# The low part of a layer's activation taken from PSUM, on VectorE in every step

## The chip, the cores and the metric

One core of a Trainium2 chip runs the program. The metric is device time in microseconds; three runs of the kernel before gave 1035.62, 1037.53 and 1037.84 us, a median of 1037.53. The engines are named as the profile names them: PE (TensorE, with PEld for its weight loads), DVE (VectorE), ACT (ScalarE), POOL (GpSimd) and SP (SyncE, which issues the DMAs).

## The reference

A recurrent attention (`r`, `k`, `v`, `w`, `u`; 4 batches, 8 heads, 768 positions, 48 per head) gives 3072 tokens of 384 values. Two feed-forward layers follow, each 384 to 2048 to 384:

```python
h = x @ w_in
g = np.where(h >= 1, h, np.where(h <= -1, 0.0, (h + 1) ** 2 / 4))   # layer 1
y = g @ w_out
h = y @ w2_in
g = h * (1.0 / (1.0 + np.exp(-1.702 * h)))                          # layer 2
out = g @ w2_out
```

The weights arrive as float64 bits, and all is computed in float32. Each matrix product is made of three products of rounded parts: an operand is split into a high part, rounded to the matmul's type (`gh` for the activation), and a low part, the rest (`gl = g - gh`).

## The kernel before, in words

The tokens are cut into 8 tiles of 384, and the 2048 hidden values into 16 slices of 128. A **step** `s` is one slice of one tile: 128 steps of layer 1, then 128 of layer 2 (`step`, line 260). A step issues, in the order of the program:

- `gemm1` (L651): nine matmuls into a PSUM tile `hp`, the slice of `h`. Up to step 111 there are two `hp` buffers, so that `gemm1` of step s needs the buffer of step s-2 to be free; from step 112 there are four.
- the first half of the activation. In layer 1 (`relu2_a`) DVE clamps `hp` into an SBUF tile `t` (L688), and ACT squares `t` (L689); in layer 2 ACT alone takes the sigmoid (L707).
- `low_g` of step s-1 (L676): `gl = t - gh`. It goes to POOL and DVE in turn, step by step.
- one slot of attention work for the tile after this one: a window of 128 tokens passes through some twenty slots. Its DVE work is two scans (L423, L425), a copy and a product (L429, L430), a reduction (L451), two predicated copies (L474) and four small updates (L510); PE has transposes, scores and products for it (L464, L469, L498, L504); POOL has products and a selection.
- `gemm2` or `gemm3` of step s-3: nine matmuls that read `gh` and `gl` of that step (L660, L669).
- the second half of the activation. In layer 1 (`relu2_b`) DVE takes the maximum of `t` and `hp` (L701) into `t`, in layer 2 their product (L712); then ACT writes `gh`, the rounded copy of `t` (L682).
- in six steps of a tile, the conversion of a piece of layer 2's weights (two DVE instructions, L638 and L642, then ACT, POOL and a DMA), and in every other step a second slot of attention work.

A tile of steps holds three windows of attention. The attention of the first tile and steps 0 to 15 are ordered by a scheduler with its own costs; from step 16 on (`manual_schedule`) each engine takes its instructions in the order of the program, and an instruction that waits holds up all that stands behind it on its engine. Attention slots end with step 111; the last tile of layer 1 (steps 112 to 127) prepares layer 2's weights instead.

Who frees `hp` before the change: the last reader is the maximum (L701).

Of the kernel before, what the change touches and what calls it, by code (L numbers as in the profile page):

```python
# [9 lines left out]
F32 = mybir.dt.float32  # L10
# [3 lines left out]
AF = mybir.ActivationFunctionType  # L14
ALU = mybir.AluOpType
# [44 lines left out]
PRIO = True  # L60
WTS = ('wt', 'gh', 'wt', 'gl', 'wt', 'ev')
WBS = ('wb', 't')
LOW0 = (0, 1)
XL_N = 6
F0 = 0
WP0 = 400
# [5 lines left out]
BANKS = (0, 1, 2)  # L72
TAGB = {'wt': 4, 'gh': 4, 'gl': 3, 'ev': 3, 'wb': 2, 't': 3}
AHEAD = 6
LOW_E = (0, 1)
GAPS = (1, 1, 1)
GAP0 = 4
CONV0 = 2
# [23 lines left out]
def fast_path(st, tc, rkw_t, nat, v_l, w1, w2, u, out, x2_d, w2_d, flag_i, force):  # L102
    nc = tc.nc
    one = st.enter_context(tc.tile_pool(name="one", bufs=1))
    p2 = st.enter_context(tc.tile_pool(name="p2", bufs=2))
# [44 lines left out]
    def to_f32(l, n):  # L150
        todo = []
        for _ in range(n):
            i = nconv[l]
            nconv[l] += 1
            raw = staged.pop((l, i))
            tags = (WTS[i % len(WTS)], WBS[i % len(WBS)]) if l == 0 and i < N0 else ("wt", "wb")
            t = p2.tile([128, DM], I32, tag=tags[0], name="wt", bufs=TAGB[tags[0]])
            b = p2.tile([128, DM], I32, tag=tags[1], name="wb", bufs=TAGB[tags[1]])
            todo.append((i, raw[:, :, 1].bitcast(I32), raw[:, :, 0], t, b))
        wide(nc, [x[1:] for x in todo])  # L160
        for i, top, low, t, b in todo:
            if l == 1 or not CHECK_LATE:
                check_w(l, i, top)
            load_w(l)
        return [(x[0], x[3].bitcast(F32)) for x in todo]

    def split_w(i, wf):
        f, q = pieces[i]
        nc.scalar.activation(out=whi[f][q], in_=wf, func=AF.Copy)
        pat = LO0 if i < N0 else LO1  # L170
        how = pat[i % len(pat)]
        if how == "p":
            ps = hooks["ps"]()
# [11 lines left out]
    def conv_w1():  # L185
        new = to_f32(0, 2) if nconv[0] < NPC else []
        if nconv[0] <= N0:
            half.extend(new)
            new = []
        while half:  # L190
            split_w(*half.pop(0))
        half.extend(new)
# [26 lines left out]
    gq = {}  # L219
# [6 lines left out]
    def where(s):  # L226
        if s < KF * len(TILES):
            return (0, s // KF, s % KF) + TILES[s // KF]
        s -= KF * len(TILES)
        return (1, s // KF, s % KF) + TILES2[s // KF]  # L230
# [29 lines left out]
    def step(s):  # L260
        if s < NS:
            l, i, f, t0, n = where(s)
            last = l == 0 and i == len(TILES) - 1
            slots = l == 0 and not last
            if l == 0 and f == 0:
                cur[0] = i
            if l == 0 and i == 0:
                with hooks["prio"](CP1):
                    while nconv[0] < min(NPC, 2 * f + 2 + AHEAD):
                        conv_w1()  # L270
                    if nconv[0] == NPC:
                        conv_w1()
            hp = pools["h"][s % len(pools["h"])].tile([128, 512], F32, tag="h", name="hp")
            gemm1(nc, hp, n, xh[l, i], xl[l, i], f, win, whi, wlo)
            if l == 0 and ALT[f % len(ALT)] and i < ALT_N:
                t = relu2_c(nc, p2, hp, n, (None, nc.gpsimd, nc.vector)[ALT[f % len(ALT)]])
            else:
                t = (relu2_a, swish_a)[l](nc, p2, hp, n)
        if s - 1 in gq:
            low_g((nc.gpsimd, nc.vector)[(LOW_E if s >= 16 else LOW0)[s % len(LOW_E)]], p2, gq, s - 1, where(s - 1)[4])  # L280
        if s < NS:
            if slots:
                per = KF - F0 if i == 0 else KF
# [22 lines left out]
        if s < NS:  # L306
            gq[s] = (relu2_b, swish_b)[l](nc, p2, t, hp, n)
# [362 lines left out]
            i += 1  # L670


def low_g(eng, p2, gq, f, n):
    t, gh, _ = gq[f]
    gl = p2.tile([128, TN], F32R, tag="gl", name="gl", bufs=3)
    eng.tensor_tensor(out=gl[:, 0:n], in0=t[:, 0:n], in1=gh[:, 0:n].bitcast(F32), op=ALU.subtract)  # L676
    gq[f] = gh, gl


def high_g(nc, p2, t, n):  # L680
    gh = p2.tile([128, TN], F32R, tag="gh", name="gh", bufs=4)
    nc.scalar.activation(out=gh[:, 0:n], in_=t[:, 0:n], func=AF.Copy)  # L682
    return t, gh, None


def relu2_a(nc, p2, hp, n):
# [11 lines left out]


def relu2_b(nc, p2, t, hp, n):  # L700
    nc.vector.tensor_tensor(out=t[:, 0:n], in0=t[:, 0:n], in1=hp[:, 0:n], op=ALU.max)  # L701
    return high_g(nc, p2, t, n)


def swish_a(nc, p2, hp, n):
# [3 lines left out]


def swish_b(nc, p2, t, hp, n):
    nc.vector.tensor_tensor(out=t[:, 0:n], in0=t[:, 0:n], in1=hp[:, 0:n], op=ALU.mult)  # L712
    return high_g(nc, p2, t, n)


def relu2(nc, t, h):
# [147 lines left out]
```

## Time and profile before

| | |
|---|---|
| median of three runs | 1037.53 us |
| the profiled execution, its own time | 1035.07 us |
| its span | 1033.3 us |
| PE busy | 950.6 us (92%) |
| DVE busy | 604.1 us (58%) |
| ACT busy | 517.5 us (50%) |
| POOL busy | 469.6 us (45%), of which 132.0 us are 128 `gl` (L676) |
| `gl` on DVE (L676) | 81.4 us, 128 of them |
| `gh` on ACT (L682) | 133.9 us, 256 of them |

The shares are means over stages of different kinds: the attention of the first tile and the first steps up to about 170 us, steps 16 to 111 with attention beside them up to about 570 us, then the last tile of layer 1 and layer 2. They are read by stage. Starts in a timeline are us from the start of the span; "[0.53 <-DVE t L701]" at the end of a row means that the engine sat idle for 0.53 us before it, and that the instruction of line 701 on DVE ended that. On DVE and ACT an instruction may start up to 0.1 us ahead of the end of the one in front of it.

### The profile page before, as it was taken

To read this page: it belongs to the slowest core of one execution; us is meant where nothing else is said; L and a number is where in the kernel's file an instruction comes from. 1 tells how busy PE (TensorE), PEld (TensorE's weight loads), DVE (VectorE), ACT (ScalarE), POOL (GpSimd) and SP (SyncE) were. 2 spreads that over 40 slices of the span, in tenths; PEclk is the share of its full clock that TensorE was granted. 3 is DMA by queue.
4 is the path that set the end of the run, shared out by engine and by line. 5 is a ranking of instruction groups with operands and counts; after the bars stand their busy time and mean duration, and the time that the engine had idled before them with its cause. 6 is when DMAs were issued, how large, how long until landed. Compare 5 with 4: busy or idle time off the path is not lost.

```text
span 1033.3 us, 18712 instructions
## 1 busy us (share of the span) xinstructions
PE 950.6 (92%) x6976; PEld 903.7 (87%) x6976; DVE 604.1 (58%) x1007; ACT 517.5 (50%) x1221; POOL 469.6 (45%) x481
## 2 busy tenths in 40 slices
PE   4645889999999999999999999999999999999997
PEld 2434769989888988898989999999999999999997
DVE  8999984787877777778674663323232323232321
ACT  5654554565555655546653565455555433333332
POOL 6897872676676666766662342111111111111111
PEclk8756989999999999999999999999999999999999
DMA  9763422644534545434310543232323110101000
GB/s 250 203 191 107 129 56 56 188 126 128 145 103 110 147 129 142 131 103 126 101 43 5 167 153 108 62 107 62 108 62 109 30 46 1 47 2 46 15 9 27
DMA packets 52228, 100.20 MB, mean 97 GB/s; under 512 B 8608, under 2 KB 34464, under 8 KB 52128
## 3 DMA queue, kind: packets, MB, share of 16 engines
q1 hardware_dynamic: 52128, 98.91, 33.2%
q8 instruction: 57, 0.93, 0.4%
q14 instruction: 43, 0.35, 0.1%
HBM read 81.97 MB, written 15.73 MB: 95 GB/s over the span
## 4 chain that ended last, share of the span: by engine, by line
PE 57%; DVE 17%; POOL 8%; ACT 6%; issue 6%; DMA 4%; SPq 2%; POOLq 0%; ACTq 0%; DVEq 0%
PE hp L651 27%; PE acc L669 20%; PE acc L660 8%; DVE pi L423 2%; DVE t L701 2%; ACT gh L682 2%; DVE ra L474 2%; DVE pi L425 2%; DVE gl L676 1%; DVE wt L638 1%; DMA wst<-w 1%; POOL ra L437 1%; POOL rkn L426 1%; POOL wt L644 1%; DVE wt L642 1%
## 5 line engine op out<-in xcount | busy, mean ns | idle before, releaser
L676 POOL TENSOR_TENSOR gl<-t,gh 128x384 fp32r<-128x384 f32 x128 | 132.0, 1031 | 387.7 <-ACT gh L682 386.1
L682 ACT ACTIVATE gh<-t 128x384 fp32r<-128x384 f32 x256 | 133.9, 523 | 205.5 <-DVE t L701 122.9
L712 DVE TENSOR_TENSOR t<-t,hp 128x384 f32<-128x384 f32 x128 | 70.8, 553 | 218.6 <-ACT t L707 218.1
L707 ACT ACTIVATE t<-hp 128x384 f32<-128x384 f32 x128 | 63.0, 492 | 145.8 <-PE hp L651 145.8
L660 PE MATMUL acc<-gh,whi 128*128 128x384 f32 x384 | 132.4, 350 | 0.3 <-DVE ev L252 0.3
L660 PE MATMUL acc<-gl,whi 128*128 128x384 f32 x384 | 130.2, 339 | 1.2 <-DVE gl L676 1.2
L669 PE MATMUL acc<-wlo,gh 128*128 128x384 f32 x384 | 130.2, 339 | 0.0
L669 PE MATMUL acc<-whi,gh 128*128 128x384 f32 x384 | 129.9, 338 | 0.0
L660 PE MATMUL acc<-gh,wlo 128*128 128x384 f32 x384 | 129.6, 338 | 0.0
L669 PE MATMUL acc<-whi,gl 128*128 128x384 f32 x384 | 129.3, 337 | 0.0
L651 PE MATMUL hp<-xh,whi 128*128 128x384 f32 x384 | 95.9, 359 | 24.1 <-DVE t L701 23.0
L676 DVE TENSOR_TENSOR gl<-t,gh 128x384 fp32r<-128x384 f32 x128 | 81.4, 636 | 47.0 <-ACT gh L682 44.6
L689 ACT ACTIVATE t<-t 128x384 f32<-128x384 f32 x128 | 66.3, 518 | 78.7 <-DVE t L688 76.8
L701 DVE TENSOR_TENSOR t<-t,hp 128x384 f32<-128x384 f32 x128 | 70.1, 548 | 51.9 <-ACT t L689 51.1
L644 POOL TENSOR_TENSOR wt<-wt,wb 128x384 int32<-128x384 int32 x64 | 71.7, 1121 | 62.0 <-ACT wb L640 51.1
L651 PEld LDWEIGHTS hp<-xh,whi 128*128 128x128 f32 x384 | 67.8, 193 | 33.3 <-DVE t L701 29.9
L688 DVE TENSOR_SCALAR t<-hp 128x384 f32<-128x384 f32 x128 | 70.4, 550 | 41.7 <-PE hp L651 41.6
L651 PE MATMUL hp<-xl,whi 128*128 128x384 f32 x384 | 90.2, 344 | 0.0
L651 PE MATMUL hp<-xh,wlo 128*128 128x384 f32 x384 | 89.4, 341 | 0.0
L651 PE MATMUL hp<-x2l,whi 128*128 128x384 f32 x384 | 88.8, 339 | 0.0
L651 PE MATMUL hp<-x2h,wlo 128*128 128x384 f32 x384 | 88.0, 337 | 0.0
L651 PE MATMUL hp<-x2h,whi 128*128 128x384 f32 x384 | 87.4, 335 | 0.0
(106 smaller groups left out, 1944.3 us busy)
## 6 DMA issues: line engine op xcount, KB each, us to landing
wst<-w SPq DMA_DIRECT2D x96, 384.0 KB, 3.4
rk<-rkw_t SPq DMA_DIRECT2D x48, 289.7 KB, 4.9
rkn<-nat SPq DMA_DIRECT2D x24, 384.0 KB, 4.1
w_d<-wt SPq DMA_DIRECT2D x32, 192.0 KB, 3.3
w2f<-w_d SPq DMA_DIRECT2D x32, 192.0 KB, 2.5
vn<-nat SPq DMA_DIRECT2D x24, 192.0 KB, 3.0
lt<-v_l SPq DMA_DIRECT2D x48, 96.0 KB, 3.0
x_d<-ev SPq DMA_DIRECT2D x24, 192.0 KB, 2.5
```

The costliest lines, as they stand in the source:

```text
L423: nc.vector.tensor_tensor_scan(out=rr[:, WW:0:-1], data0=ws[:, WW:0:-1], data1=one_s[:, WW:0:-1], initial=0.0, op0=ALU.mult, op1=ALU.max)
L644: nc.gpsimd.tensor_tensor(out=t, in0=t, in1=b, op=ALU.add)
L651: nc.tensor.matmul(out=hp[:, 0:n], lhsT=win(a, f, kk), rhs=b[:, kk, 0:n], start=(i == 0), stop=(i == 3 * KD - 1))
L660: nc.tensor.matmul(out=acc[j][:, 0:n], lhsT=wout(a, f, j * 128, 128), rhs=b[:, 0:n], start=(f == 0 and i == 0), stop=(f == KF - 1 and i == 2))
L669: nc.tensor.matmul(out=o[:, 0:DM], lhsT=a[:, j * 128:(j + 1) * 128], rhs=wout(b, f, 0, DM), start=(f == 0 and i == 0), stop=(f == KF - 1 a ...
L676: eng.tensor_tensor(out=gl[:, 0:n], in0=t[:, 0:n], in1=gh[:, 0:n].bitcast(F32), op=ALU.subtract)
L682: nc.scalar.activation(out=gh[:, 0:n], in_=t[:, 0:n], func=AF.Copy)
L688: nc.vector.tensor_scalar(t[:, 0:n], hp[:, 0:n], scalar1=-1.0, scalar2=1.0, op0=ALU.max, op1=ALU.min)
L689: nc.scalar.activation(out=t[:, 0:n], in_=t[:, 0:n], func=AF.Square, bias=0.5, scale=0.5)
L701: nc.vector.tensor_tensor(out=t[:, 0:n], in0=t[:, 0:n], in1=hp[:, 0:n], op=ALU.max)
L707: nc.scalar.activation(out=t[:, 0:n], in_=hp[:, 0:n], func=AF.Sigmoid, scale=1.702)
L712: nc.vector.tensor_tensor(out=t[:, 0:n], in0=t[:, 0:n], in1=hp[:, 0:n], op=ALU.mult)
```

## The change

The result of the activation is written back into `hp`, in PSUM, by the second half (L701, L712). ACT reads `gh` from there. `low_g` reads `hp` from there too, on DVE in every step, and it is issued at the front of the next step, ahead of that step's `gemm1` and of its first half. POOL takes no `gl`. `hp` is now freed by `gl`. The two tables that dealt `gl` out between POOL and DVE are gone.

```diff
@@ step
+            if s - 1 in gq:
+                low_g(nc, p2, gq, s - 1, where(s - 1)[4])
             hp = pools["h"][s % len(pools["h"])].tile([128, 512], F32, tag="h", name="hp")
             gemm1(nc, hp, n, xh[l, i], xl[l, i], f, win, whi, wlo)
...
-        if s - 1 in gq:
-            low_g((nc.gpsimd, nc.vector)[(LOW_E if s >= 16 else LOW0)[s % len(LOW_E)]], p2, gq, s - 1, where(s - 1)[4])
+        elif s - 1 in gq:
+            low_g(nc, p2, gq, s - 1, where(s - 1)[4])
@@ low_g, high_g
-    t, gh, _ = gq[f]
+    hp, gh, _ = gq[f]
     gl = p2.tile([128, TN], F32R, tag="gl", name="gl", bufs=3)
-    eng.tensor_tensor(out=gl[:, 0:n], in0=t[:, 0:n], in1=gh[:, 0:n].bitcast(F32), op=ALU.subtract)
+    nc.vector.tensor_tensor(out=gl[:, 0:n], in0=hp[:, 0:n], in1=gh[:, 0:n].bitcast(F32), op=ALU.subtract)
...
-    nc.scalar.activation(out=gh[:, 0:n], in_=t[:, 0:n], func=AF.Copy)
+    nc.scalar.activation(out=gh[:, 0:n], in_=hp[:, 0:n], func=AF.Copy)
@@ relu2_b (swish_b alike, with mult)
-    nc.vector.tensor_tensor(out=t[:, 0:n], in0=t[:, 0:n], in1=hp[:, 0:n], op=ALU.max)
-    return high_g(nc, p2, t, n)
+    nc.vector.tensor_tensor(out=hp[:, 0:n], in0=t[:, 0:n], in1=hp[:, 0:n], op=ALU.max)
+    return high_g(nc, p2, hp, n)
```

Line numbers of the changed kernel that lie between line 75 and `low_g` are lower by two in part: L176 and L250 there are L178 and L252 before; L638 to L712 are the same.

**DVE, first scan place of a tile (layer 1, from step 16 on).** L423 to L425 are a window's scans, L429 and L430 its copy and product, L688 the clamp of a step, L701 its maximum, L676 its `gl`. Before:

```order
L425 SCALAR_TENSOR_TENSOR pi<-rk_160,seed 128x520
L701 TENSOR_TENSOR t<-t,hp 128x384
L688 TENSOR_SCALAR t<-hp 128x384
L676 TENSOR_TENSOR gl<-t,gh 128x384
L429 COPY pcs<-pi 128x8
L430 TENSOR_TENSOR rk_160<-rk_160,pi 128x512
L701 TENSOR_TENSOR t<-t,hp 128x384
L638 TENSOR_SCALAR wt<-wst 128x384
L642 SCALAR_TENSOR_TENSOR wt<-wst,wt 128x384
L451 TENSOR_REDUCE bb<-rkn 128x8
L688 TENSOR_SCALAR t<-hp 128x384
```

With the change:

```order
L425 SCALAR_TENSOR_TENSOR pi<-rk_160,seed 128x520
L701 TENSOR_TENSOR hp<-t,hp 128x384
L676 TENSOR_TENSOR gl<-hp,gh 128x384
L688 TENSOR_SCALAR t<-hp 128x384
L429 COPY pcs<-pi 128x8
L430 TENSOR_TENSOR rk_160<-rk_160,pi 128x512
L701 TENSOR_TENSOR hp<-t,hp 128x384
L638 TENSOR_SCALAR wt<-wst 128x384
L642 SCALAR_TENSOR_TENSOR wt<-wst,wt 128x384
L451 TENSOR_REDUCE bb<-rkn 128x8
L676 TENSOR_TENSOR gl<-hp,gh 128x384
L688 TENSOR_SCALAR t<-hp 128x384
```

Before, the clamp of the next step stood behind the maximum, and `gl` of every other step behind that clamp. Now `gl` stands directly behind the maximum whose value it takes, or behind the maximum, the weight piece and the reduction, and the clamp of the next step behind `gl`.

**DVE, second scan place of a tile**, where the scans are in a step's second slot, behind its maximum. Before:

```order
L701 TENSOR_TENSOR t<-t,hp 128x384
L638 TENSOR_SCALAR wt<-wst 128x384
L642 SCALAR_TENSOR_TENSOR wt<-wst,wt 128x384
L510 TENSOR_TENSOR us<-lt_162,kv_2208 48x192 x2
L423 SCALAR_TENSOR_TENSOR pi<-rk_161,one_s 128x520
L424 RECIPROCAL seed<-pi 128x8
L425 SCALAR_TENSOR_TENSOR pi<-rk_161,seed 128x520
L688 TENSOR_SCALAR t<-hp 128x384
L429 COPY pcs<-pi 128x8
L430 TENSOR_TENSOR rk_161<-rk_161,pi 128x512
L701 TENSOR_TENSOR t<-t,hp 128x384
```

With the change:

```order
L701 TENSOR_TENSOR hp<-t,hp 128x384
L638 TENSOR_SCALAR wt<-wst 128x384
L642 SCALAR_TENSOR_TENSOR wt<-wst,wt 128x384
L510 TENSOR_TENSOR us<-lt_162,kv_2208 48x192 x2
L423 SCALAR_TENSOR_TENSOR pi<-rk_161,one_s 128x520
L424 RECIPROCAL seed<-pi 128x8
L425 SCALAR_TENSOR_TENSOR pi<-rk_161,seed 128x520
L676 TENSOR_TENSOR gl<-hp,gh 128x384
L688 TENSOR_SCALAR t<-hp 128x384
L429 COPY pcs<-pi 128x8
L430 TENSOR_TENSOR rk_161<-rk_161,pi 128x512
L701 TENSOR_TENSOR hp<-t,hp 128x384
```

Before, the clamp of the next step was the first activation work behind the scans. Now it is the `gl` of the step whose maximum stands ahead of them.

**DVE, end of the part that the scheduler orders.** `ra_1376` and `ra_1377` are the predicated copies of one window, and the rows around them are steps of the first tile. Before:

```order
L178 TENSOR_TENSOR wlo_0_137<-wt,whi_0_105 128x384
L429 COPY pcs<-pi 128x8
L688 TENSOR_SCALAR t<-hp 128x384
L701 TENSOR_TENSOR t<-t,hp 128x384
L688 TENSOR_SCALAR t<-hp 128x384
L701 TENSOR_TENSOR t<-t,hp 128x384
L474 COPY_PREDICATED ra_1376<-mask,sc 64x512
L474 COPY_PREDICATED ra_1377<-mask,sc 64x512
L676 TENSOR_TENSOR gl<-t,gh 128x384
L688 TENSOR_SCALAR t<-hp 128x384
```

With the change:

```order
L425 SCALAR_TENSOR_TENSOR pi<-rk_161,seed 128x520
L474 COPY_PREDICATED ra_1376<-mask,sc 64x512
L688 TENSOR_SCALAR t<-hp 128x384
L642 SCALAR_TENSOR_TENSOR wt<-wst,wt 128x384
L474 COPY_PREDICATED ra_1377<-mask,sc 64x512
L676 TENSOR_TENSOR gl<-hp,gh 128x384
L176 TENSOR_TENSOR wlo_0_137<-wt,whi_0_105 128x384
L701 TENSOR_TENSOR hp<-t,hp 128x384
L537 TENSOR_TENSOR xl<-xr,xh 128x3x128
L676 TENSOR_TENSOR gl<-hp,gh 128x384
```

Ahead of the copy into `ra_1377` stand eleven maxima before (those of steps 0 to 10), and six with the change (0 to 5). The order of ACT is the same from step 16 on; POOL's loses its 128 `gl` and keeps the rest.

## Rows read from the trace of the kernel before

**Rows 1.** Windows: length; busy us (instructions) of PE, PEld, DVE, ACT, POOL; PEclk, DMA, GB/s.

```profile
130.00:156.00 26.00, 20.87 (x153) 18.20 (x152) 22.00 (x33) 13.57 (x30) 17.89 (x17) 0.87 0.24 56
300.00:400.00 100.00, 95.94 (x859) 89.38 (x858) 77.18 (x133) 54.74 (x136) 66.98 (x69) 1.00 0.45 124
700.00:800.00 100.00, 100.00 (x571) 100.00 (x570) 31.40 (x54) 51.95 (x130) 15.99 (x16) 1.00 0.28 87
```

**Rows 2.** Longest waits of PE, whole run, then 150 to 650 us.

```profile
PE hp L651 <- DVE t L701: 23.0, 22, 5.0
...
PE hp L651 <- DVE t L701: 10.7, 17, 1.2
```

**Rows 3.** Three lines of VectorE: duration ns min/median/max, first and last start.

```profile
L676 DVE TENSOR_TENSOR gl<-t,gh x128: 526/558/1379, 102.0 to 1018.4; 128x384 fp32r<-128x384 f32 x128
...
L701 DVE TENSOR_TENSOR t<-t,hp x128: 525/553/556, 99.6 to 615.3; 128x384 f32<-128x384 f32 x128
...
L688 DVE TENSOR_SCALAR t<-hp x128: 524/550/559, 97.9 to 613.9; 128x384 f32<-128x384 f32 x128
```

**Rows 4.** Timeline, first scan place of a tile: VectorE, then ScalarE, then PE.

```profile
327.70 0.56 DVE L701 TENSOR_TENSOR t<-t,hp 128x384 f32<-128x384 f32 x1
...
328.90 1.14 DVE L676 TENSOR_TENSOR gl<-t,gh 128x384 fp32r<-128x384 f32 x1 [0.18 <-ACT gh L682]
...
333.43 0.55 DVE L688 TENSOR_SCALAR t<-hp 128x384 f32<-128x384 f32 x1
...
328.35 0.53 ACT L682 ACTIVATE gh<-t 128x384 fp32r<-128x384 f32 x1 [4.91 <-DVE t L701]
...
328.31 0.80 PE L651 MATMUL hp<-xh,whi 128*128 128x384 f32 x3 [0.53 <-DVE t L701]
...
332.24 0.80 PE L651 MATMUL hp<-xh,whi 128*128 128x384 f32 x3 [0.51 <-DVE t L701]
```

**Rows 5.** Timeline, second scan place: VectorE, then PE.

```profile
345.42 0.56 DVE L701 TENSOR_TENSOR t<-t,hp 128x384 f32<-128x384 f32 x1
...
351.26 0.56 DVE L688 TENSOR_SCALAR t<-hp 128x384 f32<-128x384 f32 x1
...
348.89 0.69 PE L651 MATMUL hp<-xh,whi 128*128 128x384 f32 x3
...
353.19 0.80 PE L651 MATMUL hp<-xh,whi 128*128 128x384 f32 x3 [0.96 <-DVE t L701]
```

**Rows 6.** Timeline, third scan place: VectorE, then ScalarE, then PE.

```profile
373.56 0.55 DVE L701 TENSOR_TENSOR t<-t,hp 128x384 f32<-128x384 f32 x1
...
375.35 0.55 DVE L688 TENSOR_SCALAR t<-hp 128x384 f32<-128x384 f32 x1
...
375.99 0.53 ACT L689 ACTIVATE t<-t 128x384 f32<-128x384 f32 x1 [0.77 <-DVE t L688]
...
378.17 0.51 ACT L682 ACTIVATE gh<-t 128x384 fp32r<-128x384 f32 x1
...
374.38 0.69 PE L651 MATMUL hp<-xh,whi 128*128 128x384 f32 x3
...
377.54 0.69 PE L651 MATMUL hp<-xh,whi 128*128 128x384 f32 x3
```

**Rows 7.** Timeline of PE where it waits for GpSimd.

```profile
364.36 0.33 PE L504 MATMUL yt<-ra,lt 128*64 128x64 f32 x2 [0.77 <-POOL lt L446]
...
364.95 0.68 PE L504 MATMUL yt<-ra,lt 128*64 128x64 f32 x14 [0.26 <-POOL lt L446]
```

**Rows 8.** Timeline of VectorE, the last scan of the loop.

```profile
523.83 1.77 DVE L423 TENSOR_TENSOR_SCAN pi<-rk,one_s 128x520 f32<-128x520 f32 x1
```

**Rows 9.** Timeline near step 16: VectorE, then PE.

```profile
153.36 1.54 DVE L474 COPY_PREDICATED ra<-mask,sc 64x512 f32<-64x512 int32 x2
...
142.54 1.33 PE L651 MATMUL hp<-xh,whi 128*128 128x384 f32 x3 [3.71 <-DVE t L701]
...
171.56 0.79 PE L651 MATMUL hp<-xh,whi 128*128 128x384 f32 x3
```

More of the change, by code (lines that the diff above doesn't have):

```diff
@@ L62 @@
 WBS = ('wb', 't')
-LOW0 = (0, 1)
 XL_N = 6
@@ L74 @@
 AHEAD = 6
-LOW_E = (0, 1)
 GAPS = (1, 1, 1)
@@ L670, in gemm3, with low_g, high_g @@
             i += 1
-def low_g(eng, p2, gq, f, n):
-    t, gh, _ = gq[f]
+def low_g(nc, p2, gq, f, n):
+    hp, gh, _ = gq[f]
     gl = p2.tile([128, TN], F32R, tag="gl", name="gl", bufs=3)
-    eng.tensor_tensor(out=gl[:, 0:n], in0=t[:, 0:n], in1=gh[:, 0:n].bitcast(F32), op=ALU.subtract)
+    nc.vector.tensor_tensor(out=gl[:, 0:n], in0=hp[:, 0:n], in1=gh[:, 0:n].bitcast(F32), op=ALU.subtract)
     gq[f] = gh, gl
-def high_g(nc, p2, t, n):
+def high_g(nc, p2, hp, n):
     gh = p2.tile([128, TN], F32R, tag="gh", name="gh", bufs=4)
-    nc.scalar.activation(out=gh[:, 0:n], in_=t[:, 0:n], func=AF.Copy)
-    return t, gh, None
+    nc.scalar.activation(out=gh[:, 0:n], in_=hp[:, 0:n], func=AF.Copy)
+    return hp, gh, None
 def relu2_a(nc, p2, hp, n):
@@ L711, in swish_b @@
 def swish_b(nc, p2, t, hp, n):
-    nc.vector.tensor_tensor(out=t[:, 0:n], in0=t[:, 0:n], in1=hp[:, 0:n], op=ALU.mult)
-    return high_g(nc, p2, t, n)
+    nc.vector.tensor_tensor(out=hp[:, 0:n], in0=t[:, 0:n], in1=hp[:, 0:n], op=ALU.mult)
+    return high_g(nc, p2, hp, n)
 def relu2(nc, t, h):
```

## The prediction

> **What bounds the kernel now.** I read the busy time by stretch first, since the whole run mixes stages. In layer 2 PE is busy for the whole of its 100 us and VectorE for 31.40; in the attention steps (300 to 400 us) PE has 95.94, VectorE 77.18 and GpSimd 66.98; in the early stretch VectorE has 22.00 of 26 and PE 20.87 [rows 1]. So the end is set by PE, and what counts is how long PE stands still before about 570 us. Whatever it loses there comes out at the end, since layer 2 has nothing to win back. The list of waits names the one wait of PE that this change touches: gemm1 waits for the maximum on VectorE, the last reader of `hp`, 22 times, 23.0 us, 10.7 of it in 17 waits after 150 us [rows 2]. The timeline then shows where: behind a window's scans, when VectorE is late.
>
> **The loop.** With two `hp` buffers gemm1 of step s may start when step s-2 has let go of its buffer. That ended with the maximum. Now ACT's `gh` and VectorE's `gl` come behind it. The prices are in one place: a maximum starts at 327.70 and takes 0.56, `gh` starts at 328.35 and takes 0.53, and `gl` starts 0.02 after that [rows 4]. `gl` itself I take at 0.55, below. From the end of the maximum to the end of `gl` is 0.09 + 0.53 + 0.02 + 0.55 = 1.19 us. A step without attention takes PE 3.16 us (377.54 less 374.38 [rows 6]), and the buffer is asked for two steps later, so 1.19 us is covered where VectorE is on time. Where gemm1 already waits for the maximum, all of it shows. VectorE also can no longer use the wait for `gh`: the clamp of the next step used to stand in it, and now stands behind `gl`.
>
> **The price of a `gl` from PSUM.** No row shows this form, nor a VectorE result written to PSUM. The nearest: the clamp, which reads `hp` in PSUM, 524/550/559 ns; the maximum, with one input in PSUM, 525/553/556; `gl` now, both inputs in SBUF, 526/558 and up to 1379 [rows 3]. I take 0.55 for it, and the same for the maximum as before; the ends are 0.52 and 0.56. [...]
>
> **What each tile pays.** A tile of steps holds three windows, with their scans in three places. I walk each with the durations of the timeline and the order of the change.
>
> First place. The maximum ended at 328.26 and gemm1 started at 328.31. Now `gl` runs from 328.90 to 329.45 and gemm1 starts at 329.50: 1.19 late. The clamp behind it starts 1.2 later than now, but the old `gl` there took 1.14 [rows 4], and without it VectorE reaches the window's copy at the time it does today. The next `gl` stands where a clamp now starts, at 333.43, behind the maximum, the weight piece and the reduction: it ends at 333.98, and gemm1 starts at 334.03 instead of 332.24 [rows 4]. PE is 1.79 late.
>
> Second place. The maximum at 345.42 is followed by the weight piece, the updates and both scans, and the next clamp starts at 351.26 [rows 5]. The `gl` of that maximum is now in the clamp's place, so the buffer, free at 345.98 today, is free at 351.81. gemm1 starts at 351.86 instead of 348.89, 2.97 late. The step after it waited for VectorE at 353.19 today; PE, pushed back, gets there at 351.86 + 3.16 = 355.02, about when its own `gl` is ready. Net 1.83.
>
> Third place. Behind the maximum at 373.56 come the copy and the product, and the clamp at 375.35 [rows 6]. With `gl` in the clamp's place gemm1 starts at 375.95 instead of 374.38, 1.57 late. The clamp and the square behind it are 0.47 later. From that square to its `gh` ACT has 2.18 us of attention work (375.99 to 378.17 [rows 6]), so `gh` ends at 379.15, `gl` at 379.72, and gemm1 starts at 379.77 instead of 377.54: 2.23.
>
> What comes back: PE waits 0.77 and 0.26 us for GpSimd's update of the state [rows 7]; GpSimd has one `gl` less ahead of it there, 1.03 us (132.0 us for 128 in the table above), so I take all 1.03 off.
>
> Together 1.79 + 1.83 + 2.23 - 1.03 = 4.82 us a tile. The delays add up, since the places are steps apart and VectorE's own chain shifts with PE. The bounds: 1.8 if only the first place counts and the other two are absorbed, 7.0 if the second keeps its whole 2.97 and GpSimd gives nothing back. I take 4.8, nearest to the rows. The attention steps are six tiles; five hold all three places, the last only the first one (its scan at 523.83 is the last of the loop [rows 8]). 5 x 4.82 + 1.79 = 25.9 us.
>
> **The early part** is VectorE's. Its work hardly changes: eight `gl` more at 0.55, and those that were stretched are shorter. But `hp` is held longer, and the scheduler lets the steps fall back: ahead of the last window's second predicated copy stand six maxima instead of eleven. The copies start at 153.36 today [rows 9]; with five maxima and four clamps fewer ahead of them, some 0.5 us each, they end at about 149 to 150, and the `gl` that frees gemm1 of step 7 comes at about 147.5 to 149.5 (the lower figure if the copies go up as the order has them, straight behind the scan). From there to step 16 are nine steps at 3.16 us and 0.7 us of attention products, 29.1: step 16 at 176.6 to 178.6, instead of 171.56 [rows 9]. Against that, GpSimd has eight `gl` less in a stretch where it is nearly as full as VectorE. I take +5, with 0 and +7 as ends.
>
> **What costs nothing.** From step 112 on there are four `hp` buffers, two steps more of cover, and VectorE is at 31.40 of 100 us in layer 2 [rows 1]; another 16 `gl` of 0.55 in that stretch make it about 40. `gl` of each step is ready about two steps ahead of the matmuls that read it. If that cover went, each step would pay up to the 1.19, 128 of them: nothing points to that. The three `gl` buffers make a `gl` wait for PE's matmuls of three steps before; those end before PE starts the step whose clamp follows, so they hold nothing up. GpSimd's freed 132 us lie off the path but for the 1.03 above. No DMA and no queue is moved.
>
> **Sum.** 25.9 + 5 = 30.9 us. The profiled execution took 1035.07 us, which gives 1066.0. The median of the runs stands 2.46 above it, so I forecast **1068**. The bounds together give 5 x 1.8 + 1.8 + 0 = 10.8 (1048 on the median) and 5 x 7.0 + 1.8 + 7 = 43.8 (1081).
>
> **The rivals.**
> *Faster: GpSimd was the brake.* A VectorE instruction with two SBUF inputs is stretched when GpSimd works beside it: the old `gl` goes up to 1379 ns, the maximum, with one input in PSUM, never above 556 [rows 3]. If GpSimd's `gl` are what makes VectorE late, its lateness goes away with them, and with it PE's 10.7 us of waits after 150 us: 1027. That decides if VectorE gets more than 1.19 us earlier at the first place; the shorter `gl` gives 0.59 there, and GpSimd's long products beside it stay. [...] Chance 0.06.
> *No difference:* every added wait falls into time in which PE has its own queue, and the early part stays. The 17 waits speak against it. Chance 0.03, 1037.
> *Half of it:* only the first place counts. Chance 0.17, about 1048.
> *The clock as well.* [...] Chance 0.12.
> *That the change does not do what it says* is excluded by the order: GpSimd has no `gl` left. My forecast itself gets 0.62.
>
> **Numbers.** The range runs from 1046 to 1085, from just under the half case to just over the clock case; it leaves out the faster and the unchanged case and some tails. About 0.2% (2 us) is what a measurement can tell from no change. Slower by more: 0.62 + 0.17 + 0.12, less a little for small outcomes, 0.90; within: 0.03; faster: 0.07.
>
> **What would show it.** Right: PE's waits for gemm1 now name `gl` (L676) on VectorE and come to some 40 us or more after 150 us; the last scan of the loop starts near 523.83 + 5 + 24.1 = 553 us; step 16 starts at about 177; `gl` rows are 0.55 throughout; layer 2 has the same length. Wrong: gemm1 waits of under 15 us in the attention steps, a `gl` far from 0.55, or PE gaps in layer 2.

## The result, and the profile after

The changed kernel takes 1051.92 us (1050.43 to 1052.33); beside it, on the same chip, the kernel before took 1037.68. The ratio is 1.0139 with an interval of 1.0121 to 1.0157: 14.2 us slower. The direction was forecast and the time lies in the range, but 1068 put the move at over twice its size (30.5 us). The profiled execution of the changed kernel took 1052.25 us.

The page, busy times and two groups (`line engine op out<-in xcount | busy, mean ns | idle before, releaser`):

```profile
PE 955.0 (91%) x6976; PEld 905.5 (86%) x6976; DVE 647.7 (62%) x1135; ACT 511.6 (49%) x1221; POOL 326.4 (31%) x353
...
L676 DVE TENSOR_TENSOR gl<-hp,gh 128x384 fp32r<-128x384 f32 x256 | 142.1, 555 | 131.5 <-ACT gh L682 128.0
L682 ACT ACTIVATE gh<-hp 128x384 fp32r<-128x384 f32 x256 | 124.8, 488 | 170.1 <-DVE hp L701 91.4
```

GpSimd lost its 132 us of `gl`, and VectorE has 256 of them. The windows, beside [rows 1] (length; busy of PE, PEld, DVE, ACT, POOL; PEclk, DMA, GB/s):

```profile
130.00:156.00 26.00, 22.53 (x156) 20.55 (x157) 20.39 (x37) 10.99 (x23) 15.65 (x15) 0.87 0.21 51
...
300.00:400.00 100.00, 93.55 (x866) 86.79 (x865) 75.89 (x141) 55.21 (x138) 48.08 (x56) 0.98 0.43 118
...
700.00:800.00 100.00, 100.00 (x570) 100.00 (x569) 39.90 (x69) 51.21 (x131) 0.00 (x0) 1.00 0.26 84
```

Layer 2 is as full of PE as before, so nothing is lost there. The loop fell from 95.94 to 93.55 busy, though VectorE is not fuller in it (75.89 after 77.18): it stands in other waits, not in more work. The granted clock there is 0.98 and not 1.00, which the last part takes up. PE's waits, the whole run and 150 to 650 us (us in total, times, longest), against [rows 2]:

```profile
PE hp L651 <- DVE gl L676: 31.8, 41, 3.2
...
PE hp L651 <- DVE gl L676: 28.3, 39, 2.0
```

The releaser is now `gl`, as the change has it, and 10.7 us in 17 waits have become 28.3 in 39, 17.6 us more. That this is near the 17.2 by which the profiled executions differ (1052.25 less 1035.07) is chance: PE's waits for GpSimd, 5.3 us in that stretch before, are gone, and PE is busy 4.4 us longer for the same 6976 matmuls (955.0 after 950.6), in part by a lower clock in two tiles (0.65 and 0.77 in the windows of the last part). VectorE's own waits, 180 to 600 us, before:

```profile
DVE t L688 <- PE hp L651: 28.8, 27, 2.2
DVE gl L676 <- ACT gh L682: 11.3, 28, 1.1
```

and after:

```profile
DVE gl L676 <- ACT gh L682: 46.8, 63, 2.0
...
DVE t L688 <- PE hp L651: 6.8, 19, 1.1
```

VectorE stands 35.5 us longer for ACT's `gh`, and waits 22 us less for PE's `gemm1`: that was its slack, in which it had been ahead of PE.

The scans show the pace of the tiles (VectorE's timeline, first scan place of tiles 1, 2, 3 and the end), before:

```profile
190.46 1.63 DVE L423 TENSOR_TENSOR_SCAN pi<-rk,one_s 128x520 f32<-128x520 f32 x1
...
257.51 1.77 DVE L423 TENSOR_TENSOR_SCAN pi<-rk,one_s 128x520 f32<-128x520 f32 x1
...
324.00 1.77 DVE L423 TENSOR_TENSOR_SCAN pi<-rk,one_s 128x520 f32<-128x520 f32 x1
```

and after:

```profile
189.75 1.77 DVE L423 TENSOR_TENSOR_SCAN pi<-rk,one_s 128x520 f32<-128x520 f32 x1
...
261.15 1.77 DVE L423 TENSOR_TENSOR_SCAN pi<-rk,one_s 128x520 f32<-128x520 f32 x1
...
329.75 1.77 DVE L423 TENSOR_TENSOR_SCAN pi<-rk,one_s 128x520 f32<-128x520 f32 x1
...
539.37 1.77 DVE L423 TENSOR_TENSOR_SCAN pi<-rk,one_s 128x520 f32<-128x520 f32 x1
```

The loop starts 0.71 us earlier than before, not later. Its first tile takes 71.40 instead of 67.05, the next 68.60 instead of 66.49, and the end comes 15.54 later than in [rows 8]: the five tiles lose 16.25 us.

Where in a tile? The starts of `gemm1`, step by step, after less before, give the delay that PE carries; these are its changes at five places (f is the step in its tile; the first two places are parted at f 7 in tiles 1 and 2, at f 8 in the others):

| | tile 1 | 2 | 3 | 4 | 5 | mean | forecast |
|---|---|---|---|---|---|---|---|
| first scan place (f 6 to 8) | 1.01 | 0.72 | 0.43 | 0.41 | 0.43 | 0.60 | 1.79 |
| copies of a window (f 9, 10) | 2.07 | 0.73 | 0.75 | 0.98 | 0.75 | 1.06 | none |
| second scan place (f 11 to 14) | 1.57 | 1.59 | 2.59 | 1.59 | 2.36 | 1.94 | 1.83 |
| comes back (to f 0 of the next tile) | -1.39 | -2.34 | -1.42 | -2.34 | -1.39 | -1.78 | -1.03 |
| third scan place (f 1, 2) | 1.26 | 1.63 | 1.43 | 1.64 | 1.59 | 1.51 | 2.23 |

They come to 3.33 a tile, 16.66 us; with -0.71 ahead of them and 1.40 in the last tile PE carries 17.35 us into layer 2, and the same 17.35 to its end.

The first place after, the timeline of VectorE and then PE, to be read against [rows 4]:

```profile
333.45 0.56 DVE L701 TENSOR_TENSOR hp<-t,hp 128x384 f32<-128x384 f32 x1
334.62 0.56 DVE L676 TENSOR_TENSOR gl<-hp,gh 128x384 fp32r<-128x384 f32 x1 [0.61 <-ACT gh L682]
335.10 0.55 DVE L688 TENSOR_SCALAR t<-hp 128x384 f32<-128x384 f32 x1
335.56 0.38 DVE L429 COPY pcs<-pi 128x8 f32<-128x8 f32 x1
...
338.25 0.55 DVE L676 TENSOR_TENSOR gl<-hp,gh 128x384 fp32r<-128x384 f32 x1
...
335.24 0.80 PE L651 MATMUL hp<-xh,whi 128*128 128x384 f32 x3 [1.33 <-DVE gl L676]
...
338.86 0.80 PE L651 MATMUL hp<-xh,whi 128*128 128x384 f32 x3 [0.18 <-DVE gl L676]
```

From the end of the maximum (334.01) to the end of `gl` (335.18) are 1.17 us: the price of 1.19 was right. But PE's wait grew by 0.80 only, from 0.53 to 1.33, since VectorE is 0.4 us less late against PE here than before (the part on the prediction tells why). The second `gl` then costs no more: behind it PE waits 0.18, where it had waited 0.51.

The second place, VectorE, ScalarE, PE, against [rows 5]:

```profile
351.75 0.56 DVE L701 TENSOR_TENSOR hp<-t,hp 128x384 f32<-128x384 f32 x1
...
357.77 0.56 DVE L676 TENSOR_TENSOR gl<-hp,gh 128x384 fp32r<-128x384 f32 x1
...
361.33 0.56 DVE L676 TENSOR_TENSOR gl<-hp,gh 128x384 fp32r<-128x384 f32 x1 [0.56 <-ACT gh L682]
...
352.68 0.49 ACT L682 ACTIVATE gh<-hp 128x384 fp32r<-128x384 f32 x1 [1.05 <-DVE hp L701]
...
358.38 1.00 PE L651 MATMUL hp<-xh,whi 128*128 128x384 f32 x3 [2.02 <-DVE gl L676]
...
363.19 0.69 PE L651 MATMUL hp<-xh,whi 128*128 128x384 f32 x3
```

`gh` is ready at 353.17; `gl` starts at 357.77, since both scans stand ahead of it. In the even tiles no small updates (L510) stand between the weight piece and the scans, and in tile 4 the first scan takes 1.23 where it took 1.79 in tile 3; the same wait is short there:

```profile
427.64 0.80 PE L651 MATMUL hp<-xh,whi 128*128 128x384 f32 x3 [0.57 <-DVE gl L676]
```

### The profile page after: what moved, and what is told of

Read it like the earlier page. It is cut to its first block, busy times and chain, and to the rows that moved or that the text cites. A ratio compares the mean times of both kernels' runs of the same rounds, so it can differ in the third digit from the quotient of the medians.

```text
span 1050.5 us, 18721 instructions
## 1 busy us (share of the span) xinstructions
PE 955.0 (91%) x6976; PEld 905.5 (86%) x6976; DVE 647.7 (62%) x1135; ACT 511.6 (49%) x1221; POOL 326.4 (31%) x353
## 4 chain that ended last, share of the span: by engine, by line
PE 62%; DVE 17%; issue 6%; ACT 6%; DMA 5%; POOL 2%; SPq 2%; ACTq 0%; POOLq 0%; DVEq 0%
PE hp L651 30%; PE acc L669 19%; PE acc L660 8%; DVE pi L423 2%; DMA wst<-w 2%; DVE gl L676 2%; DVE ra L474 2%; DVE hp L701 2%; DVE t L688 2%; ACT gh L682 2%; PE sc L469 1%; SPq L525 1%; DVE wt L638 1%; DVE us L510 1%; DVE wt L642 1%
## 5 line engine op out<-in xcount | busy, mean ns | idle before, releaser
L676 DVE TENSOR_TENSOR gl<-hp,gh 128x384 fp32r<-128x384 f32 x256 | 142.1, 555 | 131.5 <-ACT gh L682 128.0
L682 ACT ACTIVATE gh<-hp 128x384 fp32r<-128x384 f32 x256 | 124.8, 488 | 170.1 <-DVE hp L701 91.4
L712 DVE TENSOR_TENSOR hp<-t,hp 128x384 f32<-128x384 f32 x128 | 71.9, 562 | 157.5 <-ACT t L707 156.9
L689 ACT ACTIVATE t<-t 128x384 f32<-128x384 f32 x128 | 67.0, 523 | 139.6 <-DVE t L688 138.4
L701 DVE TENSOR_TENSOR hp<-t,hp 128x384 f32<-128x384 f32 x128 | 71.6, 559 | 56.1 <-ACT t L689 54.2
L660 PEld LDWEIGHTS acc<-gh,whi 128*128 128x128 f32 x384 | 72.3, 190 | 9.0 <-ACT gh L682 6.5
L688 DVE TENSOR_SCALAR t<-hp 128x384 f32<-128x384 f32 x128 | 70.2, 549 | 9.3 <-PE hp L651 9.0
```

The source lines that it names most:

```text
L660: nc.tensor.matmul(out=acc[j][:, 0:n], lhsT=wout(a, f, j * 128, 128), rhs=b[:, 0:n], start=(f == 0 and i == 0), stop=(f == KF - 1 and i == 2))
L676: nc.vector.tensor_tensor(out=gl[:, 0:n], in0=hp[:, 0:n], in1=gh[:, 0:n].bitcast(F32), op=ALU.subtract)
L682: nc.scalar.activation(out=gh[:, 0:n], in_=hp[:, 0:n], func=AF.Copy)
L688: nc.vector.tensor_scalar(t[:, 0:n], hp[:, 0:n], scalar1=-1.0, scalar2=1.0, op0=ALU.max, op1=ALU.min)
L689: nc.scalar.activation(out=t[:, 0:n], in_=t[:, 0:n], func=AF.Square, bias=0.5, scale=0.5)
L701: nc.vector.tensor_tensor(out=hp[:, 0:n], in0=t[:, 0:n], in1=hp[:, 0:n], op=ALU.max)
```

## The experiments

All kernels but the last two and the one with `gl` first are the kernel before with three switches (those with a third buffer have two pools changed besides): whether a step keeps its value in PSUM, whether `gl` stands ahead of the next step's `gemm1` (else it stays behind that step's clamp), and which engine takes it.

```diff
+            if s - 1 in gq and in_front(s - 1):
+                low_g(eng_g(s), p2, gq, s - 1, where(s - 1)[4])
             hp = pools["h"][s % len(pools["h"])].tile([128, 512], F32, tag="h", name="hp")
...
-            gq[s] = (relu2_b, swish_b)[l](nc, p2, t, hp, n)
+            gq[s] = (relu2_b, swish_b)[l](nc, p2, t, hp, n, hp if in_ps(s) else t)
```

With `in_ps` and `in_front` true everywhere that is the changed kernel. In these kernels the lines stand 13 lower: `gl` is L689, the maximum L714, the clamp L701, `gemm1` L664, `gh` L695 (15 lower in the last two and in the one with `gl` first). "Loop" below is the time from the scans of the first of sixteen windows to those of the last, in the profiled execution (333.37 us before, 349.62 after); two kernels with the same loop gave 332.4 and 335.3, so differences under some 3 us in it say little. Each was timed in five rounds beside the kernel before.

**The early part and the loop apart.**

```diff
+def in_ps(s):
+    return s < 16
+def in_front(s):
+    return s < 16
```

> The changed form in steps 0 to 15 alone; every later step as before. Theory A (the early part loses nothing with the change; in the changed kernel's trace step 21 starts 0.7 us earlier than before): 1035 to 1038.5 us. Rival (the early part loses what the prediction took for it, 5 us, and something in the attention steps gives it back): 1041 to 1044.

Measured 1032.94 us, ratio 0.9964 (0.9951 to 0.9978): 3.4 us faster than before, and the best of all kernels here. The loop is unchanged (333.2). The early part of the change is a gain, where I had forecast a loss of 5.

```diff
+def in_ps(s):
+    return s >= 16
+def in_front(s):
+    return s >= 16
```

> The changed form from step 16 on alone; steps 0 to 15 as before. Theory A (all of the loss is in the attention steps): 1051 to 1055 us. Rival: 1045 to 1048.

Measured 1055.24, ratio 1.0184 (1.0164 to 1.0204): 19.0 us slower, with a loop of 349.7. Less the 3.4 that is 15.6, against 14.2 for both together: the two parts about add up, and the loss is the loop's.

**Load, place and hold apart.** The change does three things to `gl` in the loop: all of it on VectorE, ahead of the next clamp, and `hp` held until it is done. First the load alone, from SBUF, at the old place:

```diff
-            low_g((nc.gpsimd, nc.vector)[(LOW_E if s >= 16 else LOW0)[s % len(LOW_E)]], p2, gq, s - 1, where(s - 1)[4])
+            low_g(nc.vector, p2, gq, s - 1, where(s - 1)[4])
```

> The kernel before, with gl on VectorE in every step: from SBUF, behind the next step's clamp, hp freed by the maximum. Theory H (the loss comes from hp being held until gl): at most 1042 us. Theory L (the loss comes from 128 more gl on VectorE): 1047 or more.

Measured 1036.24, ratio 1.0001 (0.9990 to 1.0012). That line of VectorE (duration ns min/median/max, first and last start):

```profile
L689 DVE TENSOR_TENSOR gl<-t,gh x256: 536/558/1370, 102.4 to 1021.7; 128x384 fp32r<-128x384 f32 x128
```

So 128 more `gl` on VectorE, some of them stretched, cost nothing at the old place, behind the next clamp.

Then the place as well, still from SBUF, with `hp` let go by the maximum (`in_ps` false, `in_front` true, all on VectorE):

```diff
+def in_front(s):
+    return True
-            low_g((nc.gpsimd, nc.vector)[(LOW_E if s >= 16 else LOW0)[s % len(LOW_E)]], p2, gq, s - 1, where(s - 1)[4])
+            low_g(nc.vector, p2, gq, s - 1, where(s - 1)[4])
```

> The kernel before, with gl on VectorE in every step and in front of the next step's gemm1 and clamp as in the change, but from SBUF, so that hp is freed by the maximum. Theory H (hold of hp): at most 1043 us. Theory F (the place of gl, whose wait for gh holds up the clamp): 1048 or more.

Measured 1067.91, ratio 1.0298 (1.0284 to 1.0312): 31.6 us, more than the whole change costs. VectorE's `gl` and PE's longest wait, 180 to 640 us:

```profile
L689 DVE TENSOR_TENSOR gl<-t,gh x256: 528/559/1554, 102.3 to 1054.1; 128x384 fp32r<-128x384 f32 x128
...
PE hp L664 <- DVE t L714: 31.0, 22, 2.7
```

PE still waits for the maximum, and three times as long as before: the clamp, the square, the maximum and the next `gh` are one chain through VectorE and ACT, and a `gl` in front of the clamp puts its wait for `gh` into that chain (46.9 us of it in 180 to 600 us, against 13.6 with the load alone). From SBUF the `gl` is also longer (mean 666 ns, 555 in the changed kernel), and it is now on the path. How the 31.6 divides between the place and the stretching these runs don't say; the same stretched `gl` behind the clamp cost nothing.

Then the hold without the place (`in_ps` true, `in_front` false):

```diff
+def in_ps(s):
+    return True
+def in_front(s):
+    return False
```

> The changed kernel with gl put back behind the next step's clamp: VectorE in every step, from hp in PSUM, so hp is still held until gl. Theory H (the hold of hp costs: gl at the second scan place would come behind the scans and the clamp): 1046 to 1056 us. Theory F (the place of gl ahead of the clamp costs, the hold is covered): 1033 to 1041.

Measured 1048.26, ratio 1.0102 (1.0084 to 1.0121): 11.0 us. Loop 344.7, against 332.4 with the load alone. PE's wait, 180 to 640 us:

```profile
PE hp L664 <- DVE gl L689: 27.1, 22, 2.0
```

So the hold of two buffers until `gl` costs some 11 us without any change of place, and the place adds 3.7 to it (1.0139 against 1.0102; in the loop alone 4.9, 349.62 against 344.7). The two are not a sum, since 11.0 and 31.6 would be 42.6; they delay the same `gemm1`, and the PSUM form has the short `gl`.

**`gl` as early as can be.** From step 16 on directly behind the maximum, ahead of the weight piece and the second slot:

```diff
             gq[s] = (relu2_b, swish_b)[l](nc, p2, t, hp, n, hp if in_ps(s) else t)
+            if 16 <= s:
+                low_g(nc.vector, p2, gq, s, n)
```

> The changed kernel with gl directly behind the maximum from step 16 on, ahead of the weight piece and the second slot. Theory H (the buffer comes free earlier at the second scan place): 1043 to 1049 us. Theory F (VectorE waits for gh some 0.6 us in every step with nothing else to do): 1052 or more.

Measured 1069.65, ratio 1.0317 (1.0301 to 1.0332). VectorE's wait, 180 to 600 us, against 46.8 in 63 for the change:

```profile
DVE gl L691 <- ACT gh L697: 70.6, 94, 1.8
```

The weight pieces and second slots had covered 24 us of that wait. Here an early `gl` that VectorE must wait for is worse than a late one. Part of the loss can be PE's clock: the granted clock of 180 to 640 us is 0.97 in this run, where it was 1.00 before (0.951 over the whole profiled execution, against 0.963), and 0.03 of these 460 us are an estimated 14 us of full rate lost at most.

**A third buffer.** To take the hold away, three `hp` buffers, paid with one of the three PSUM buffers of the attention; first the kernel before, then the change, then `gl` behind the clamp.

```diff
-    ps_h = st.enter_context(tc.tile_pool(name="ps_h", bufs=2, space=PSUM))
+    ps_h = st.enter_context(tc.tile_pool(name="ps_h", bufs=3, space=PSUM))
...
-        ps_s = sa.enter_context(tc.tile_pool(name="ps_s", bufs=3, space=PSUM))
+        ps_s = sa.enter_context(tc.tile_pool(name="ps_s", bufs=2, space=PSUM))
```

From step 112 on there are four again, three and one where it was two and two.

> The kernel before with three hp buffers up to step 111, the third taken from the attention's PSUM pool (two tiles instead of three). It is the base of the next two. Its waits of PE for the maximum go; the attention may lose by its smaller pool: 1030 to 1045 us.

Measured 1061.21, ratio 1.0236 (1.0221 to 1.0250): with a third `hp` buffer and one buffer less for the attention it is 24.3 us slower. PE's longest wait is no longer for `hp`, it is in the attention's products, 180 to 640 us:

```profile
PE yt L517 <- issue: 25.2, 12, 3.3
```

"issue" says that the profile shows nothing that PE waited for. The same stretch as a window (columns as in [rows 1]):

```profile
180.00:640.00 460.00, 428.31 (x3611) 409.31 (x3610) 310.36 (x550) 242.55 (x599) 262.64 (x280) 0.96 0.40 112
```

The granted clock is 0.96, where it was 1.00 before: of these 460 us that is an estimated 18 us of full rate lost at most, so much of the 24.3 can be the clock behind those waits, and not the waits themselves. (The profiled execution is the slowest of the five, 1065.36.)

> The changed kernel with the same three buffers. Theory H (hp held until gl is what costs): within 5 us of e7_before_3h, since the buffer is asked for a step later. Theory F (the chain of clamp, maximum, gh and gl on VectorE has become too long for a step): 9 us or more above e7_before_3h.

Measured 1079.88, ratio 1.0412 (1.0397 to 1.0427): 18.7 above the run before it. PE does not wait for `hp`, yet the same wait in the attention has grown:

```profile
PE yt L517 <- issue: 37.6, 14, 3.8
```

> e5_psum_behind (gl from PSUM on VectorE, behind the next clamp) with the same three buffers. Theory H: within 3 us of e7_before_3h. Rival (something else in reading gl from PSUM costs): 8 us or more above it.

Measured 1055.27, ratio 1.0169 (1.0151 to 1.0187): 5.9 below the kernel before with three buffers. With the hold covered by a third buffer the PSUM form at the old place costs nothing, and even gains (GpSimd has no `gl` in it either, which may be the gain); with `gl` in front it costs 18.7. So there are two causes, hold and place, and each is enough for a loss: the hold 11.0 with two buffers, the place 18.7 with three, and 31.6 from SBUF with two. With this division of PSUM the wait sits elsewhere, so these three tell of the sign, and not of sizes in the kernel with two buffers.

**The early form with all `gl` on VectorE behind the clamp** (`in_ps` and `in_front` for s < 16, after that SBUF at the old place):

```diff
+def in_front(s):
+    return s < 16
-            low_g((nc.gpsimd, nc.vector)[(LOW_E if s >= 16 else LOW0)[s % len(LOW_E)]], p2, gq, s - 1, where(s - 1)[4])
+            low_g(nc.vector, p2, gq, s - 1, where(s - 1)[4])
```

> The changed form in steps 0 to 15, then gl from SBUF on VectorE in every step behind the next clamp, hp freed by the maximum; GpSimd takes no gl. From e1_early_only and e3_dve_all, which made 1032.9 and no change: 1031 to 1034 us. Rival: what the early part won depended on the rest: 1036 to 1038.

Measured 1034.63, ratio 0.9978 (0.9968 to 0.9988): 2.2 us faster than before, not better than the early form alone. GpSimd's relief does not show in the loop (335.3, and 332.4 in the run with the load alone).

**Is the wait at the second scan place what a tile loses?** There `gh` is ready 4.6 us ahead of its `gl`. In step 9 of each tile `gl` goes behind the weight piece, ahead of the second slot:

```diff
                     conv_w2()
+            if s >= 16 and slots and f == 9:
+                low_g(nc.vector, p2, gq, s, n)
             if slots:
```

> The changed kernel, but in one step of each tile (f = 9, from step 16 on) gl is issued behind the weight piece and ahead of the second slot with its scans, instead of behind the scans. In the changed kernel's tile from 329 us the maximum ended at 352.31, gh ran from 352.68 to 353.17 and the weight piece to 353.38, so this gl can run at 353.4 with hardly a wait, and frees the buffer at about 353.9 instead of 358.33. Theory A, VectorE's own chain holds the next step as well: gemm1 of step 11 loses its wait of 2.02, but gl of step 10, whose clamp and maximum stand behind the same scans, ends some 0.5 us earlier only (361.4 instead of 361.9), and gemm1 of step 12 waits for it instead. Then a tile gains about 0.5, the tile with the reduced clock some 1.8, together 2 to 4 us: 1048 to 1050. Theory B, the wait at the second place is what a tile loses there: 2.02 + 1.82 + 1.83 in the odd tiles, 2 x 0.57 in the even ones and 1.6 for the clock come back, 8.4 us: about 1043.5. Theory C, one gl more ahead of the scans makes all of VectorE's chain later by 0.55: no gain or a loss.

Measured 1051.73, ratio 1.0145 (1.0131 to 1.0160): the same as the change (1.0139). The timeline at the same place, VectorE and then PE:

```profile
351.47 0.55 DVE L691 TENSOR_TENSOR gl<-hp,gh 128x384 fp32r<-128x384 f32 x1
...
358.40 0.56 DVE L691 TENSOR_TENSOR gl<-hp,gh 128x384 fp32r<-128x384 f32 x1 [0.56 <-ACT gh L697]
...
354.38 0.69 PE L666 MATMUL hp<-xh,whi 128*128 128x384 f32 x3
...
359.02 0.80 PE L666 MATMUL hp<-xh,whi 128*128 128x384 f32 x3 [1.31 <-DVE gl L691]
```

The `gl` is early now, and the `gemm1` that had waited 2.02 starts at 354.38 without a wait; the next one waits 1.31 instead (1.20 and 2.52 in the other odd tiles), for a `gl` that hangs on the same scans by its clamp and maximum. In the even tiles the wait moved one step on and grew (0.58 and 0.57 became 0.83 and 1.10); the first scan behind the early `gl` took 1.89 us there, where it had taken 1.23. PE's waits for `gl` come to 29.0 us (27.9 in the change, 180 to 640 us). So theory B falls: the scans on VectorE hold two steps in a row, and freeing the first buffer only moves the wait. The 2 to 4 us of theory A did not come either; the time is that of theory C, no gain.

The same with the other steps' `gl` behind the clamp, and the changed form up to step 15 (`in_ps` true everywhere):

```diff
+def in_front(s):
+    return s < 16
...
+            if s >= 16 and slots and f == 9:
+                low_g(nc.vector, p2, gq, s, n)
```

> The changed form for steps 0 to 15; from step 16 on the value is taken from PSUM with gl behind the next step's clamp, as in the run with gl behind the clamp (11.0 us above before), but in step 9 of each tile ahead of the second slot with its scans. The early form is worth 3.4 us by its own run. At the second place that run waited 1.79, 1.99 and (at 450 us and later) 1.82 and about 1.8 in odd places, 0.5 in even ones. Theory A (VectorE's chain holds the next step as well): a tile gains 0.5 to 0.7, so 1048.3 - 3.4 - 3 = about 1042. Theory B (the wait is the loss): 1048.3 - 3.4 - 6.5 = about 1038.5. If the hold of the buffer is paid mostly here, it ends within 2 us of before.

Measured 1043.33, ratio 1.0062 (1.0044 to 1.0081). That is 0.0040 under the run with `gl` behind the clamp (1.0102), of which the early form's 0.0036 is the most; the loop went from 344.7 to 342.8. It is near theory A's 1042, and still some 6 us slower than before: PE waits 1.26 and 0.66 us at the first scan place and 1.81 at the third in each tile, where the hold is as before.

## Why the prediction was right or wrong

**What bounds the kernel: right.** PE's gaps before layer 2 set the end, and layer 2 neither gave nor took: 17.35 us of delay at its start and at its end.

**The mechanism of the loop: right.** `hp` is freed by `gl`, 1.17 us behind the maximum (forecast 1.19). PE's waits name `gl`, and the run with only the hold, 11.0 us, shows that it is enough for most of the loss. The waits come to 28.3 us after 150 us, where I had asked for 40. What the prediction did not part is the place of `gl`: ahead of the clamp it is enough for a loss too.

**The price of a `gl`: right.** Its line (duration ns min/median/max), against [rows 3]:

```profile
L676 DVE TENSOR_TENSOR gl<-hp,gh x256: 525/557/559, 103.7 to 1038.9; 128x384 fp32r<-128x384 f32 x128
```

0.55 was forecast, 0.557 is the median; the form from SBUF has 0.558 [rows 3].

**What each tile pays: 4.82 forecast, 3.33 measured, and this is the larger part of the miss** (7.5 of 13.6 us). The step that failed is "the delays add up, since the places are steps apart and VectorE's own chain shifts with PE". It did not shift as it stood, it became shorter. Before, a `gl` that VectorE took stood behind a clamp, with its wait for `gh`. Now it stands ahead of the clamp, where VectorE had waited for PE (28.8 us before, 6.8 after). So the scans behind that clamp start nearer to PE's `gemm1` than in the rows that I walked. The second place, before:

```profile
343.19 0.55 DVE L688 TENSOR_SCALAR t<-hp 128x384 f32<-128x384 f32 x1
344.18 0.56 DVE L676 TENSOR_TENSOR gl<-t,gh 128x384 fp32r<-128x384 f32 x1 [0.44 <-ACT gh L682]
...
347.71 1.61 DVE L423 TENSOR_TENSOR_SCAN pi<-rk,one_s 128x520 f32<-128x520 f32 x1
```

and after:

```profile
350.06 0.56 DVE L676 TENSOR_TENSOR gl<-hp,gh 128x384 fp32r<-128x384 f32 x1 [0.85 <-PE kv L498]
350.53 0.55 DVE L688 TENSOR_SCALAR t<-hp 128x384 f32<-128x384 f32 x1
...
354.05 1.79 DVE L423 TENSOR_TENSOR_SCAN pi<-rk,one_s 128x520 f32<-128x520 f32 x1
```

From the clamp to the scan are 4.52 us before and 3.52 after. By place, in the table above:

- *First place, 1.79 forecast, 0.60 measured.* VectorE met PE 0.4 us less late: the maximum starts 3.67 behind the `gemm1` ahead of it (333.45 less 329.78), where it was 4.06 (327.70 less 323.64). The 0.4 lies at the small updates (L510) ahead of the scans, which wait 0.16 us for GpSimd where they had waited 0.45. And the copy L429 of 8 values took 0.38 instead of the 1.16 that it had between 329.96 and 331.12 before, which I had carried over (0.38 to 0.39 at this place in all six tiles, 1.15 to 1.16 before), so that the second `gl` was ready with only 0.18 to wait for.
- *Second place, 1.83 forecast, 1.94 measured.* The wait was 2.02 and not 2.97, since the scan starts 6.41 behind the `gemm1` two steps ahead (354.05 less 347.64), where it was 7.27 (347.71 less 340.44). But in tiles 3 and 5 a step at a lower clock followed (told in the last part). That the mean was right is luck, by two errors that cancel: it is 1.6 in the three tiles at full clock, and 2.4 to 2.6 in the two.
- *Third place, 2.23 forecast, 1.51 measured*, again since VectorE is less late: the maximum starts 1.94 behind `gemm1` (381.53 less 379.59), where it was 2.46 (373.56 less 371.10). The `gl` that stood between clamp and scan at 369.50 is gone from there. PE waits 0.89 and 0.30, not 1.57 and 0.66.
- *What comes back, 1.03 forecast, 1.78 measured.* PE's waits for GpSimd are gone as forecast. In the even tiles a wait of 0.67 for the maximum, before, was covered by the delay as well; I had walked an odd tile only.
- *Left out:* a fourth place, behind the two predicated copies, where a `gl` now stands: PE waits 0.5 to 0.7 there in four tiles, 1.8 in the first, and a tile loses 1.06.

**The early part: +5 forecast, -0.7 in the profiled executions, -3.4 by the run that has only this part.** The step that failed is the time of the copies: I took 153.36 and subtracted the VectorE time of five maxima and four clamps, 4.5 us. The timeline after, VectorE and then PE, against [rows 9]:

```profile
140.91 0.72 DVE L474 COPY_PREDICATED ra<-mask,sc 64x512 f32<-64x512 int32 x1
...
134.87 1.33 PE L651 MATMUL hp<-xh,whi 128*128 128x384 f32 x3 [3.16 <-DVE gl L676]
...
142.29 0.79 PE L651 MATMUL hp<-xh,whi 128*128 128x384 f32 x3
...
170.49 0.81 PE L651 MATMUL hp<-xh,whi 128*128 128x384 f32 x3 [0.40 <-DVE gl L676]
```

The last copy ends at 141.63, not at 149 to 150. Before, it stood behind the maximum of step 10, and that maximum waits for PE and ACT: taking five steps from ahead of it takes away their whole turns, not 0.5 us each. The scans of that stretch run earlier as well: the second one (L425) starts at 137.58, where it was 144.91, and the first no longer waits 2.32 us for its DMA. How much each gives was not parted. Step 7 therefore starts at 142.29; from there to step 16 it is 28.20 us (29.1 forecast), at 170.49 instead of about 177. The clock gave nothing back: from 84.80 to 171.50 us the granted clock is 0.86 after and 0.89 before. Why the scheduler's order with the PSUM form gains 3.4 and not less was not tried further. Step 21 started at 190.49 before and at 189.78 with the change; with `gl` in front from SBUF, in the run above, at 191.25, and with `gl` from PSUM behind the clamp at 191.96. So neither the place nor the PSUM form alone gives it.

**The last tile: 1.79 forecast, 1.40 measured**, and near by luck: its first place costs about 0.5, and the rest comes in f 8 to 10, where I had put nothing. **The offset of 2.46** between the profiled execution and the median was wrongly carried over: the changed kernel's profiled execution lies at its own median, 1052.25 against 1051.92.

**The sum:** 7.5 (tiles) + 5.7 (early part) + 0.4 (last tile) are the 13.6 us by which the profiled executions differ less than forecast, and the 2.46 is the rest.

**The rivals.** GpSimd was not the brake: with all `gl` on VectorE and nothing else changed the time is the same (1.0001), not 1027. PE's waits for GpSimd fell from 5.3 to 0.3 us there, those for the maximum rose from 10.1 to 13.2. "Half of it" named the better time (1048) by the wrong reason: it is not that only the first place counts, all do, each for less. The clock case came in two of the five tiles (3 and 5): the granted clock fell to 0.50 for a part of a step, and that step took 4.81 us instead of 3.16, 1.65 more. The range, up to 1085, leaves room for 3.16 more in each of the five tiles; no run shows that term.

## What to carry to other kernels

A result that stays in PSUM is not free storage: whatever reads it last frees the buffer, and with two buffers an added 1.2 us behind the old last reader was charged to the matmuls wherever the engine was late (11.0 us here). On an engine that takes its instructions in order, the place of a dependent read counts for more than its length: 128 more of them cost nothing behind the next step's clamp, and 11 to 32 us when they held the buffer or stood ahead of it. To free one buffer earlier gained nothing where the next one hung on the same scans. When delays at several places are added up, take an instruction out of the place that it leaves as well as adding it where it goes, look for waits into which it now falls, and time a moved instruction by the chain behind which it stood, never by the busy time on its own engine.

## What the runs showed of the hardware

The clock behind a wait. Behind the wait of 2.02 us in tile 3, the step ran slower (window, columns as above):

```profile
358.30:363.20 4.90, 4.82 (x19) 4.81 (x20) 4.21 (x9) 2.31 (x5) 2.98 (x3) 0.65 0.03 7
...
499.00:506.00 7.00, 7.00 (x33) 7.00 (x32) 4.78 (x10) 4.95 (x15) 2.48 (x2) 0.77 0.22 64
```

A mean granted clock of 0.65 (0.50 from 359.00 to 362.00), and 4.81 us from this `gemm1` to the next where a step takes 3.16. The second window lies in tile 5: behind a wait of 1.83 at 497.50 the first matmuls kept their 0.80, then the clock fell (0.50 from 499.00 to 502.00), and the next `gemm1` came 4.81 us on as well. Behind a wait of 1.82 at 219.58 in tile 1 it did not fall: the granted clock of tile 1 is 1.00. So waits of nearly the same length had either outcome. Before the change the granted clock of 165 to 580 us is 1.00.

VectorE beside GpSimd. With one input in PSUM no `gl` of 256 is above 559 ns; with both in SBUF it goes up to 1370 and 1554 in the two runs above. In the kernel before, 21 of the 128 `gl` on VectorE took over 600 ns (657 to 1379), and beside each of them GpSimd was at work. That is not enough by itself: beside 12 others GpSimd worked for 315 to 513 ns as well, and they took 526 to 577. Of the maxima, with one input in PSUM, 87 of 128 had GpSimd beside them for over 50 ns, and of the clamps 94; none is above 556 and 559. With the change it is 84 of the 256 `gl`, at 559 or less. ACT's `gh` is also shorter from PSUM, 488 ns against 523 in the table of before. A copy of 128x8 values takes anything from 112 to 1991 ns (L429 after, 24 of them), and its median was 796 before and 890 with no `gl` left on GpSimd and the old order. It hangs on the place: at the first scan place it took 1.15 to 1.18 us in all tiles of those two kernels, and 0.38 to 0.39 in those of the change. A short instruction's time in one row is no constant to carry over to another order.
